# A decode-attention kernel: FFN and most of wo in column tiles, the loop's code moved by a block's remainder, unused matmuls in small loops

## The chip, the cores and the metric

The kernel runs on one core of one Trainium2 chip. The metric is the device time of one execution in microseconds (us), here the median of four: 660.58 (659.37 to 661.59). "The profile" is one more execution taken with the hardware profiler, and a line such as L275 is line 275 of that kernel's source. TensorE is the matmul engine (PE; its weight loads are PEld), VectorE is DVE, ScalarE is ACT, GpSimd is POOL and SyncE is SP; SP issues nearly all transfers.

## The reference

One decoding step of a transformer layer with a cached attention and a feed-forward network (FFN) side by side, both on the same normalised input. There are 2 sequences, one new token each, width 512, 32 heads of 128, 8192 cached positions, FFN width 1792, all in bf16.

```python
xn = _layernorm(x)                                   # (2, 1, 512)
q = (xn @ wq).reshape(2, 1, 32, 128)                 # per head
scores = q . k_cache * 128 ** -0.5                   # k_cache (2, 32, 8192, 128)
o = softmax(scores) . v_cache
out = x + o.reshape(2, 1, 4096) @ wo + relu(xn @ w1) @ w2
```

The two caches are 134 MB each, wq and wo 4 MB each, w1 and w2 1.8 MB each: 280.5 MB are read for 2 KB of output.

## The kernel before, in words

The 64 pairs of sequence and head are taken four at a time (`U = 4`), in `NP = 16` steps. For one step a K tile `ks` and a V tile `vs` are loaded, each 128 partitions by 64 KB (8 MB). There is one buffer of each, so K of the next step can be requested only when the transposes have read all of `ks`, and V of the next step only when the V matmuls have read all of `vs`. SP issues them in that order in `load` (L182): K waits for the semaphore `pT`, V for `sW`. The first and last K tiles, and the second and last V tiles, come in two halves.

Before the loop, x is normalised, wq is loaded into `vs`, and q is computed with 32 matmuls of 512 columns (L254). After that TensorE runs a hardware loop (`pe.Fori`) whose body is written out in full: 256 transposes of `ks` (L275) with VectorE and ScalarE copying the results to SBUF (`kT`, L429); 256 score matmuls (L282), with the maximum of each half of the scores found by VectorE (L476), transposed on TensorE (`turn`, L294) and spread to all partitions (`spread`, L300); ScalarE's exponentials (L550); 256 matmuls of V with the probabilities (L335, "PV"); and, except in the last two steps, 24 unused matmuls of 512 columns (L346) whose results nobody reads, at the end of the step.

Each step's softmax is scaled by its own maxima; the tail after the loop joins the halves. `RS` holds the sums, spread by four fp32 matmuls (L356), from which VectorE makes the factors, ending in `OTn` (L512). w1, w2 and wo are loaded into `ks`, after the last transposes: SP issues w1 (L190), w2 (L191), and wo in four pieces (L194) that follow `cuts = (0, 18, 26, 30, 32)`; a row `j` of `wo_sb` is 128 KB. TensorE first puts x into the output accumulator `fin` (L362), then does the FFN's first part with 56 matmuls, w1 as the weights and the two normalised tokens as the two moving columns (L373). It transposes `OTn` (L385), regroups it with four matmuls (L389), and then accumulates w2 (14 rows) and wo (32 rows) into `fin`, four matmuls a row with two moving columns each (`project`, L400, 184 in all). `fin` then holds the output with the 512 features spread over partitions; a copy `yT` (L526), a transpose (L420) and a copy `osb` (L528) lead to the output transfer (L196). On every engine the order is the order of the source: nothing is scheduled by a planner.

## Time and profile before

| what | value |
|---|---|
| median of 4 runs | 660.58 us |
| the profiled execution's own time | 660.51 us |
| its span, first to last instruction | 658.7 us |
| busy share of the span: PE, PEld, DVE, ACT, POOL | 90%, 82%, 40%, 44%, 1% |
| chain that ended last, by engine | DMA 49%, PE 48%, issue 1%, DVE 1% |
| DMA, mean over the span | 426 GB/s |
| mean granted TensorE clock | 0.981 |

The span is shorter than the execution's time by what lies before its first and after its last instruction. The chain is followed back from the last instruction to what released each step; it names one engine at a time, even where another ended nearly as late. "issue" is time in which an engine waited for nothing that the profile shows. Matmuls are pipelined: the duration of one record is longer than the distance from one to the next, so that costs are taken from a row's whole length divided by its count.

### The profile page before, as it was taken

How to read it: one execution, taken by the hardware profiler on the slowest of the kernel's cores; microseconds unless marked ns; L12 is line 12 of the kernel's file. 1: busy time of each engine (PE TensorE's matmuls, PEld its weight loads, DVE VectorE, ACT ScalarE, POOL GpSimd, SP SyncE). 2: the span in 40 equal slices, each digit the busy share in tenths (PEclk: the TensorE clock that was granted, in tenths of full speed). 3: DMA queues.
4: the chain of work that ended last, by engine and by line, in shares of the span. 5: the costliest groups of instructions: out<-in, count | busy, mean ns of one | idle time of the engine just before them, and what ended most of it. 6: DMA issues, size and time to landing. Idle time of an engine off the chain costs nothing.

```text
span 658.7 us, 27600 instructions
## 1 busy us (share of the span) xinstructions
PE 595.4 (90%) x12987; PEld 537.9 (82%) x12987; DVE 261.8 (40%) x503; ACT 290.7 (44%) x532; POOL 7.2 (1%) x30
## 2 busy tenths in 40 slices
PE   1876999999999899999989999998999999999997
PEld 0576897988879698887969878796987879798987
DVE  1440350716335071632507154260715416071721
ACT  1332452635445263543537354343725435372820
POOL 2000000000000000000000000000000000000000
PEclk9997898999999999999999999999999999999987
DMA  9999999999999999999999999999999999999996
GB/s 378 447 440 436 393 448 394 438 446 438 402 442 438 446 442 398 442 434 446 446 410 430 442 438 446 406 434 446 430 446 422 422 446 434 442 438 398 444 412 270
DMA packets 6223, 280.66 MB, mean 426 GB/s; under 512 B 706, under 2 KB 708, under 8 KB 964
## 3 DMA queue, kind: packets, MB, share of 16 engines
q1 hardware_dynamic: 6208, 280.50, 98.8%
q8 instruction: 8, 0.13, 0.1%
q14 instruction: 3, 0.02, 0.0%
q10 hardware_dynamic: 4, 0.00, 0.0%
HBM read 280.50 MB, written 0.00 MB: 426 GB/s over the span
## 4 chain that ended last, share of the span: by engine, by line
DMA 49%; PE 48%; issue 1%; DVE 1%; ACT 0%; SPq 0%; ACTq 0%
DMA ks<-in_A_k_cache_dram 49%; PE tp L275 34%; PE ot L335 6%; PE Sc L282 5%; PE ms L346 2%; PE Sc L400 1%; DVE mcol L476 1%; PE ms L373 1%; PE ms L294 0%; ACT L429 0%; ACT kT L429 0%; PE Sc L356 0%; PE ms L300 0%; SPq L182 0%; SPq L170 0%
## 5 line engine op out<-in xcount | busy, mean ns | idle before, releaser
L429 DVE COPY kT<-tp 128x1024 bf16<-128x1024 bf16 x320 | 209.2, 687 | 247.5 <-PE tp L275 241.8
L275 PEld LDWEIGHTS tp<-identb,ks 128*128 128x128 bf16 x4096 | 228.9, 98 | 23.6 <-DMA ks<-in_A_k_cache_dram 21.3
L275 PE MATMUL tp<-identb,ks 128*128 128x128 bf16 x4096 | 231.8, 219 | 16.7 <-DMA ks<-in_A_k_cache_dram 15.2
L429 ACT COPY kT<-tp 128x1024 bf16<-128x1024 bf16 x192 | 188.1, 1014 | 127.9 <-PE tp L275 127.9
L282 PE MATMUL Sc<-q,kT 128*128 128x64 bf16 (+8 forms) x4096 | 133.4, 191 | 4.8 <-issue 4.8
L335 PE MATMUL ot<-prm,vs 128*128 128x64 bf16 x4096 | 134.8, 195 | 2.2 <-issue 2.2
L335 PEld LDWEIGHTS ot<-prm,vs 128*128 128x128 bf16 x4096 | 130.8, 99 | 4.2 <-issue 2.3
L282 PEld LDWEIGHTS Sc<-q,kT 128*128 128x128 bf16 x4096 | 128.8, 98 | 6.3 <-issue 5.1
L346 PE MATMUL ms<-identb 128*128 128x512 bf16 x336 | 75.0, 380 | 0.0
L476 DVE TENSOR_REDUCE mcol<-Sc 32x1 bf16<-32x128 f32 x128 | 37.1, 290 | 94.4 <-PE Sc L282 93.1
L550 ACT ACTIVATE prm<-Sc,nm 32x128 bf16<-32x128 f32 x128 | 68.9, 538 | 5.4
L545 ACT COPY nm<-ms 128x4 f32<-128x4 f32 x32 | 5.2, 163 | 140.7 <-PE ms L300 140.7
L346 PEld LDWEIGHTS ms<-identb 128*128 128x128 bf16 x336 | 32.0, 98 | 36.6 <-issue 0.3
L561 ACT COPY OTf<-ot 128x8 f32 x16 | 2.6, 165 | 74.7 <-PE ot L335 74.7
L550 ACT ACTIVATION_READ_ACCUMULATOR prm<-Sc,nm x128 | 32.0, 250 | 0.0
L294 PE MATMUL ms<-identb,mcol 128*1 128x128 bf16 x32 | 7.0, 218 | 22.1 <-DVE mcol L476 22.1
L429 ACT ACT_TABLE_LOAD x16 | 20.5, 1283 | 3.7 <-issue 3.6
L294 PEld LDWEIGHTS ms<-identb,mcol 128*1 128x1 bf16 x32 | 2.5, 79 | 23.9 <-issue 23.1
L254 PE MATMUL ot<-vs,xz 128*16 128x512 bf16 x32 | 9.7, 477 | 8.8 <-DMA vs<-in_A_wq_dram 8.8
L254 PEld LDWEIGHTS ot<-vs,xz 128*16 128x16 bf16 x32 | 3.3, 106 | 14.8 <-issue 12.7
L483 DVE TENSOR_REDUCE mx<-ms 1x4 bf16<-1x128 bf16 x32 | 8.9, 279 | 13.8 <-PE ms L294 13.8
L236 POOL COPY q<-qb 128x4 bf16<-128x4 bf16 x16 | 3.0, 186 | 592.4 <-PE Sc L282 572.6
(61 smaller groups left out, 46.6 us busy)
## 6 DMA issues: line engine op xcount, KB each, us to landing
ks<-in_A_k_cache_dram SPq DMA_DIRECT2D x4, 4096.0 KB, 23.0
vs<-in_A_v_cache_dram SPq DMA_DIRECT2D x4, 4096.0 KB, 21.5
vs<-in_A_wq_dram SPq DMA_DIRECT2D x1, 4096.0 KB, 12.5
ks<-in_B_w_dram SPq DMA_DIRECT2D x2, 1792.0 KB, 16.5
ks<-in_A_wo_dram SPq DMA_DIRECT2D x1, 2304.0 KB
ks<-in_A_wo_dram SPq DMA_DIRECT2D x1, 1024.0 KB, 26.1
ks<-in_A_wo_dram SPq DMA_DIRECT2D x1, 512.0 KB, 26.9
ks<-in_A_wo_dram SPq DMA_DIRECT2D x1, 256.0 KB, 27.0
```

Source lines behind the costliest of these rows:

```text
L254: i = pe.matmul(qp, lhsT=xz[:, kt, Z - g * Bsz:Z - g * Bsz + QG * Bsz], rhs=vs[:, (kt * QG + g) * 512:(kt * QG + g + 1) * 512], start=(g = ...
L275: t = pe.transpose(tp[e % 4][:, i, :], ks[:, kk * Dh:(kk + 1) * Dh], identb[:])
L282: t = pe.matmul(Sc[:, U * kk:U * (kk + n)], lhsT=kT[e][:, i, :], rhs=rep(q4[:], n), start=True, stop=True,)
L294: pe.transpose(trp[:, i * P:(i + 1) * P], mcol[:, i:i + 1], identb[:]).then_inc(sT, 1)
L335: t = pe.matmul(oh[:, i, :], lhsT=vs[:, kk * Dh:(kk + 1) * Dh], rhs=rep(prm[:, kk, :], REP), start=(first == 0), stop=(first == KB // 2 - 1),)
L346: pe.matmul(ms[:], lhsT=identb[:], rhs=identb[:].rearrange("p (o k) -> p o k", o=1).to_broadcast([P, 4, P]), start=True, stop=True,)
L373: i = pe.matmul(hp[:, j, :], lhsT=w1_v[:, kt, j, :], rhs=xz[:, kt, Z:Z + Bsz], start=(kt == 0), stop=(kt == KT - 1),)
L400: t = pe.matmul(fin[:, k * Bsz:(k + 1) * Bsz], lhsT=w[:, j, k * P:(k + 1) * P], rhs=x[:, j, :], start=False, stop=(last and k == KT - 1),)
L429: fn(kT[e][:], tp[e % 4][:]).then_inc(kR[e % HG], 1)
L476: m = v.tensor_reduce(out=mcol[own, i:i + 1], in_=S[own, i * KB // 2:(i + 1) * KB // 2, u], axis=AX.X, op=ALU.max,)
L483: v.tensor_reduce(out=mx[:, i, :], in_=trp[:, i * P:(i + 1) * P].rearrange("o (u m) -> o u m", u=U), axis=AX.X, op=ALU.max, negate=True,). ...
L550: x = a.activation(out=prm[own, k, u], in_=S[own, k, u], func=ACTF.Exp, bias=nm[own, i, u:u + 1], scale=1.0, accum_out=RS[own, i, bass.ds( ...
```

## The change

- **Column tiles.** The FFN and rows 0 to 23 of wo change the roles of their operands. The activations become the weights, padded from 2 to `CT = 32` columns, and a row of w1, w2 or wo is moved through as 512 columns. A matmul then writes 32 output partitions, and four such outputs (`tile(ap, c)`) lie side by side in the 128 partitions of a PSUM bank. w1 takes 16 matmuls, w2 14, wo's rows 0 to 23 take 24. The hidden layer comes out with tokens along partitions, so ScalarE copies it to SBUF (`hb`), TensorE transposes it in four matmuls into `tp[3]`, and VectorE's relu writes `hT`. The sums `y` of the four column tiles are copied to SBUF in fp32 (`ys`), and four fp32 matmuls with `sel2` add the four tiles and turn them into `fin`. The last 8 rows of wo are done as before, 32 matmuls into `fin`. `hT` and `OX` are zeroed by GpSimd, as their padding is read; `OX`, `hb` and `ys` lie in the `kT` buffers, `hp` and `y` in the PSUM of the transposes.
- **Pieces.** The wo pieces are cut at 24 instead of 26.
- **50 matmuls ahead of q.** They are unused, 128 columns each, and stand before the wait for wq; the loop's code moves by 100 instructions.
- **Unused matmuls.** A step's 24 become a small hardware loop of 2 x 5, followed by one of 3 x 5 that is left out in step one: 25 in a step, 10 in step one.

The diff, without unchanged sizes and waits:

```diff
-WARM = 24
+EARLY = 50
+CT = 32
+    TC = P // CT
+    QW = 512 // P
+    first_j = [min(c * QW, FJ - QW) for c in range(TC)]
-    xz = sb([P, KT, 2 * Z + Bsz], bf16, "xz")
+    xz = sb([P, KT, max(2 * Z + Bsz, Z + CT)], bf16, "xz")
+    sel2 = sb([P, Bsz], f32, "sel2")
-    cuts = (0, 18, 26, 30, WJ)
+    cuts = (0, 18, 24, 30, WJ)
+    WIDE = 2
...
+        g.memset(hT[:], 0.0).then_inc(sI, 1)
...
+        g.wait_ge(sS, 2 * NP)
+        g.memset(OX, 0.0).then_inc(sI, 1)
...
+        for i in range(EARLY):
+            pe.matmul(ms[:, 0:P], lhsT=identb[:], rhs=identb[:], start=True, stop=True)
         pe.wait_ge(sV, 6)
         pe.wait_ge(dQ, 16)
...
+        def warm(n):
+            with pe.Fori(0, n):
+                for i in range(5):
+                    pe.matmul(ms[:], lhsT=identb[:], rhs=..., start=True, stop=True)
...
             with pe.If_lt(reg, NP - 1):
-                for i in range(WARM):
-                    pe.matmul(ms[:], lhsT=identb[:], rhs=..., start=True, stop=True)
+                warm(2)
+                with pe.If_ne(reg, 1):
+                    warm(3)
...
-        for j in range(FJ):
-            for kt in range(KT):
+        for kt in range(KT):
+            for c in range(TC):
                 i = pe.matmul(
-                    hp[:, j, :],
-                    lhsT=w1_v[:, kt, j, :],
-                    rhs=xz[:, kt, Z:Z + Bsz],
+                    tile(hp, c),
+                    lhsT=xz[:, kt, Z:Z + CT],
+                    rhs=w1_v[:, kt, first_j[c]:first_j[c] + QW, :],
...
+        pe.wait_ge(sF, 2)
+        for i in range(QW):
+            t = pe.transpose(tp[3][:, i, :], hb[:, i * P:(i + 1) * P], identb[:])
...
         for j in range(FJ):
-            project(w2_sb, j, hT)
+            c = j % TC
+            pe.matmul(
+                tile(y, c), lhsT=hT[:, slot[j], :], rhs=w2_sb[:, j, :],
+                start=(0 < j < TC), stop=False,
+            )
         pe.wait_ge(sV, 110)
-        for c in range(NC):
-            pe.wait_ge(*piece[c])
-            for j in range(cuts[c], cuts[c + 1]):
-                t = project(wo_sb, j, OX, j == WJ - 1)
+        for i in range(WIDE):
+            pe.wait_ge(*piece[i])
+            for j in range(cuts[i], cuts[i + 1]):
+                t = pe.matmul(
+                    tile(y, j % TC), lhsT=OX[:, j, :], rhs=wo_sb[:, j, :],
+                    start=False, stop=(j >= cuts[WIDE] - TC),
+                )
         t.then_inc(sH, 1)
+        for i in range(WIDE, NC):
+            if i == WIDE:
+                pe.wait_ge(sF, 5)
+                for k in range(KT):
+                    pe.matmul(
+                        fin[:, k * Bsz:(k + 1) * Bsz],
+                        lhsT=ys[:, k * P:(k + 1) * P],
+                        rhs=sel2[:],
+                        start=(k == 0),
+                        stop=False,
+                    )
...
+        v.tensor_copy(ys, y).then_inc(sF, 1)
...
+        a.wait_ge(sF, 1)
+        a.copy(hb, hp).then_inc(sF, 1)
```

On VectorE the relu moves behind the copy `Ob`, with a wait for the four transposes.

## The prediction

> **What bounds the kernel now.** I read the order of the chain of waits first, because the page's shares (DMA 49%, PE 48%) are averages over stages with different limits. From step three on, every turn of the loop is the same pair: 24.16 us waiting for a K tile, 14.48 us of transposes that set its buffer free for the next request. The stage table (its last three columns are TensorE's clock, the DMA's busy share and GB/s) and the list of waits say why:

> ```profile
> 200.00:400.00 200.00, 187.18 (x4122) 169.66 (x4120) 85.19 (x159) 94.88 (x170) 0.93 (x5) 1.00 1.00 434
> ```
> ```profile
> PE tp L275 <- DMA ks<-in_A_k_cache_dram: 15.2, 13, 1.7
> ```

> Between 200 and 400 us the DMA is never idle and moves 434 GB/s; one step is 16.8 MB (a K and a V tile of 128 x 64 KB each), which at that rate is 38.7 us, the measured turn. There the DMA is the limit, and TensorE has 15.2 / 13 = 1.2 us of slack a step. Only two stretches are not like that.

> The first is steps one and two. From the chain in order of time (start, us, what):

> ```profile
> 41.20 1.52 PE Sc L282 x49
> 42.72 1.16 issue
> 43.88 4.04 PE Sc L282 x127
> 47.91 0.15 PE ms L294
> 48.06 3.66 issue
> ...
> 63.64 2.21 issue
> 65.85 3.98 PE ot L335 x84
> 69.84 5.41 PE ms L346 x24
> 75.25 14.29 PE tp L275 x256
> ...
> 114.08 14.31 PE tp L275 x256
> ...
> 128.41 23.49 DMA ks<-in_A_k_cache_dram
> ...
> 166.44 24.16 DMA ks<-in_A_k_cache_dram
> ```

> Here TensorE is the chain. Three "issue" rows are holes in which it waits for nothing that the profile names, in its first pass through the loop only. Between two of them lie 127 score matmuls and one transpose, 128 pairs of weight load and matmul, 256 instructions. The DMA table for two stretches shows the code queue, q8 (packets, MB, share):

> ```profile
> q8 instruction: 4, 0.07, 0.8%
> ```
> ```profile
> q8 instruction: 2, 0.03, 0.7%
> ```

> The second stretch is the end (chain, the page's list of DMA issues, and the timeline's row of the four wo requests):

> ```profile
> 650.47 5.01 PE Sc L400 x184
> ```
> ```profile
> ks<-in_A_wo_dram SPq DMA_DIRECT2D x1, 1024.0 KB, 26.1
> ...
> ks<-in_A_wo_dram SPq DMA_DIRECT2D x1, 256.0 KB, 27.0
> ```
> ```profile
> 626.46 1.88 SPq L194 DMA_DIRECT2D ks<-in_A_wo_dram  x4
> ```

> The chain names TensorE alone, but the last wo piece, asked for at 627.9, lands 27.0 us later at 654.9, and the last matmul row ends at 655.48. The two end within 0.6 us of each other. A faster tail on TensorE alone can therefore win only some tenths.

> **The change part by part.**

> *Step one, 10 unused matmuls for 24.* K tile 1 was asked for at 41.23 and took 31.9 us: it lay there at 73.1, but its transposes began at 75.25, behind the unused ones (5.41 us for 24, 0.225 each). Fourteen fewer are 3.2 us, of which 2.15 are usable: then the landing is the limit. So K tile 2 is asked for near 87.4, not 89.57. What that is worth: tile 2 landed at 89.57 + 22.3 = 111.9, tile 3 at 128.41 + 23.49 = 151.9. From tile 1 that is 78.8 us for two turns where 2 x 38.7 = 77.4 would do. 1.4 us of DMA time were lost because requests came too late, and the whole stream behind, the tail too, was late by it. Bounds: 1.4 us gained; at the other end 0.3 lost, if TensorE, idle before 73.1, runs the transposes at a lower clock (the stage table has 0.75 for 50 to 70 us) and asks no earlier. I take 1.1 gained, nearer the full value, because the request moves by more than the loss.

> *The block shift.* Counting back 256 instructions at a time from the hole at 42.72, the old blocks begin 49.5 pairs into the loop; 100 new instructions put a block's first instruction at the loop's first. The loop then touches seven blocks, as before, and the one fetched ahead is the eighth. In step one a block took 7.8 us from hole to hole (43.88 to 51.72); the scores begin at 41.2 as before, and four block changes at 7 to 7.8 us put the end of PV at 69 to 72 us, a little less where a block was asked for ahead, against 69.84: no term, and ten unused matmuls still end about when tile 1 lands. The 50 matmuls themselves run from about 5 to 10 us, under the wait for wq that ends at 13.56 us: nothing; without that cover 5.3 us, at 0.107 each (a quarter of the 0.427 us between L254's first 512-column matmuls).

> *Unused matmuls in loops, 25 a step.* One more is 0.216 us (5.18 / 24) inside 1.2 us of slack: nothing. The branch: the jump into L346 at 69.84 and the jump back at 75.25 follow the row before them without idle time, so five more, each under 1.08 us of queued matmuls, cost 0; at the other end 0.15 us each (the gap at 610.05, where the loop turns with no unused matmuls), 0.75 a step, which the slack just takes. They also shorten the code.

> *Code fetches.* One more block is fetched in step one, and in the tail one or none before the last landing, for two. A block on one DMA engine (434 / 16 = 27 GB/s) is 0.6 us. [...]

> *FFN and wo in column tiles.* In the old run's time. Removed: L362 (0.18), 56 w1 matmuls (3.45), 184 narrow ones (5.01). RS ends at 645.96. Sixteen w1 matmuls of 512 columns follow; no row shows column tiles, so they are bounded by 0.216 each one after another (3.46) and a quarter of it side by side (0.86). I take the latter, as the four write different partitions with their own weights: 646.8. The copy hb on ScalarE (half of L429's 1.01) is done at 647.5. The transposes of OTn wait for VectorE's 648.20, not for w1; Ob (0.28), four transposes, the relu (0.19, now queued behind Ob on VectorE) lead to w2 at about 649.2, for 650.47 before. 14 + 18 wide matmuls take 1.7 us (to 6.9): 650.9. Now the next wait: piece 1, two rows shorter. The old one was asked for at 626.95, landed at 653.05; two rows are 256 KB, 0.6 us: 652.4. Six wide matmuls 0.32, their drain 0.17, the copy ys 0.68 (nearest row L458, 512 columns from PSUM), four fp32 matmuls 1.02 (L356, the same weight size), 32 narrow ones at 5.01 / 184 = 0.027 each 0.87. That ends at 655.5, against 655.48: the tail gains nothing by itself; I count 0.1 lost. Bounds: 0.4 gained (only the last landing counts), 1.0 lost (half clock in the tail, which the old run has from about 651 us, 0.50 in the stage table's last stretch).

> *Without cost:* sel2's reduction and the larger xz memset lie before wq's 13.4 us; the hT memset precedes a 19.7-us wait of GpSimd; the OX memset (0.95, L227's size) runs from 634 us, its reader comes at 648. SP's queue has as many requests.

> [...]

> **Rivals.**

> *The gain does not arrive.* The clock falls while TensorE waits for tile 1, K tile 2 is asked for no earlier, and the tail's chain behind piece 1 (3.1 us) shows: 660.6, up to 661.6 at half clock. For it: step one has clock 0.75 and the new wait falls there. Against: the window before the transposes still holds ten matmuls.

> *Column tiles run one after another (slower).* w1 then ends at 649.4 and w2 starts near 650.5; 38 wide matmuls take 8.2 us, and with 2.7 us of drain, copy, fp32 and narrow work the end is at 661.4, 6.0 late, 4.7 after the 1.3 gained: 665.2. From (652.7 - 649.2) / 38 = 0.09 us a wide matmul the tail loses, from 0.13 it has eaten the 1.3. For it: no row of the old run shows overlap. Against: disjoint columns and outputs.

> *The loop no longer fits.* The new block start coincides with the loop start within one or two instructions of my count. If the jump lands one instruction before it, the loop needs nine blocks with the one ahead, and if eight is all that is held (the old run needed just eight), each step costs what step one's pass did: 24.87 to 69.84 less 1.7 of waiting for K, and 5.4 of unused matmuls, is 48.7 for 38.7; 14 x 10 makes about 800.

> *The small loops cost more than the slack,* say 0.2 us a step beyond it: 14 x 0.2 = 2.8 against 1.2, 662.1.

> **How the numbers follow.** The profiled execution took 660.51 us (span 658.7 and 1.8 around it), 0.07 under the median of 660.58. -1.1 - 0.2 + 0.1 = -1.2: 659.3. A measurement of this kernel tells about 0.2%, 1.3 us, from no change, so this is just at the edge. Chances: my forecast 0.62, its own range 658.2 to 660.0; no gain 0.22; serial tiles 0.08; no fit 0.04; loop cost 0.04. Faster: 0.45 from the forecast. Same: its other 0.17 and 0.14 of the second case. Slower: 0.24. Bounds summed give -2.4 to +1.9, 658.1 to 662.4 with the median's own spread of a few tenths at the low end: 657.7 to 662.3, which leaves out the serial tiles and the loop that does not fit.

> **What would show it.** Right: transposes of tile 1 near 73.1, turns of 38.7 from tile 2 on, no q8 packets from 75 to 640 us, wide matmuls well under 0.1 us apart, fp32 rows waiting behind a copy. Wrong: wide matmuls 0.216 apart, "issue" holes in later steps, K waits shrunk to nothing, or tile 2 asked for at 89 us again.

## The result, and the profile after

The change makes the kernel a little slower. Its median is 661.84 us (42 executions, 658.6 to 664.14) against 659.72 for the kernel before (67 executions, 658.15 to 667.29), and the ratio is 1.002 with a 95% interval of 1.0011 to 1.003, that is 0.7 to 2.0 us. The medians differ by 2.1 us, the means by 1.3: of the 42 executions 9 lie at 658.6 to 659.7, the rest from 660.2 up. The forecast was 659.3, faster. The range held the time, the direction was wrong.

The profiled execution of the kernel after took 660.69 us (span 658.9), 0.2 more than the profiled one of before, and 1.2 less than its own median: it is one of the quicker ones. It shows the new wait, though not yet what that costs in most executions. Its chain in order of time (start, us, what):

```profile
41.20 3.85 PE Sc L299 x127
45.06 1.47 issue
...
50.99 2.84 issue
...
61.37 1.91 issue
63.27 4.03 PE ot L361 x128
67.30 3.38 issue
70.67 0.50 PE ot L361 x6
71.18 3.29 PE ms L324 x10
74.47 14.31 PE tp L292 x256
88.79 24.04 DMA ks<-in_A_k_cache_dram
112.88 14.48 PE tp L292 x256
...
166.05 24.16 DMA ks<-in_A_k_cache_dram
```

Before, step one had three "issue" holes, 7.0 us together. Now there are four, 9.6 us, and the new one stands before the last six PV pairs: 3.38 us of waiting for 0.50 us of work. PV therefore ends at 71.2, the ten unused matmuls at 74.5, 1.7 us after K tile 1 landed (72.8), and K tile 2 is asked for at 88.8, not at the forecast 87.4. The steady turn is unchanged (24.16 and 14.48 us), as the stage table and the list of waits say too:

```profile
200.00:400.00 200.00, 188.26 (x4132) 170.16 (x4130) 84.86 (x158) 94.52 (x170) 0.93 (x5) 1.00 1.01 435
```
```profile
PE tp L292 <- DMA ks<-in_A_k_cache_dram: 14.3, 14, 1.9
```

The code queue has five packets from 42 to 76 us, none from 76 to 655, and one after that:

```profile
q8 instruction: 5, 0.08, 0.9%
```

The tail (chain of the same kernel):

```profile
645.58 3.77 PE tp L391 x16
...
650.69 1.04 PE tp L427 x14
651.73 1.33 PE tp L435 x22
653.07 0.02 issue
653.09 0.70 DVE kT L578
653.79 0.04 issue
653.84 1.05 PE Sc L444 x8
654.89 0.81 PE Sc L454 x32
```

The 38 wide matmuls of w2 and wo take 2.4 us and the 32 narrow ones that stay 0.81, where 184 narrow ones took 5.01; the sum over the four tiles (copy, four fp32 matmuls) gives that back; and w1's 16 wide ones take 3.77, where 56 narrow ones took 3.45. The last narrow row ends at 655.70, against 655.48. Seen from the landing of the last wo piece (654.7 us, before 654.9) that is 1.0 us behind it, for 0.6 before.

**One measure serves for all runs below.** K tile 3 should land two turns, 77.4 us, after K tile 1. What it takes beyond that is DMA time lost in steps one and two. In the profile of before that was 78.81 - 77.4 = 1.41, in the one after 78.72 - 77.4 = 1.32. These two profiles thus differ by next to nothing in this measure; what the new wait costs is seen against the kernels below that lose less than 0.1, and in the other profiles with the same code shift.

### The profile page after: what moved, and what is told of

Its sections match the earlier page's. It is cut to its first block, busy times and chain, and to the rows that moved or that the text cites. A ratio compares the mean times of both kernels' runs of the same rounds, so it can differ in the third digit from the quotient of the medians.

```text
span 658.9 us, 27588 instructions
## 1 busy us (share of the span) xinstructions
PE 598.2 (91%) x12891; PEld 534.6 (81%) x12891; DVE 262.6 (40%) x505; ACT 291.3 (44%) x533; POOL 8.6 (1%) x32
## 4 chain that ended last, share of the span: by engine, by line
DMA 52%; PE 44%; issue 2%; DVE 1%; ACT 0%; SPq 0%; ACTq 0%
DMA ks<-in_A_k_cache_dram 52%; PE tp L292 34%; PE ot L361 4%; PE Sc L299 4%; PE tp L391 1%; DVE mcol L525 1%; PE ms L324 0%; PE tp L435 0%; ACT L472 0%; PE ms L311 0%; PE Sc L444 0%; PE tp L427 0%; ACT kT L472 0%; PE Sc L379 0%; PE Sc L454 0%
## 5 line engine op out<-in xcount | busy, mean ns | idle before, releaser
L361 PE MATMUL ot<-prm,vs 128*128 128x64 bf16 x4096 | 132.8, 194 | 5.3 <-issue 5.3
L361 PEld LDWEIGHTS ot<-prm,vs 128*128 128x128 bf16 x4096 | 128.6, 98 | 7.3 <-issue 5.5
## 6 DMA issues: line engine op xcount, KB each, us to landing
ks<-in_A_wo_dram SPq DMA_DIRECT2D x1, 256.0 KB, 27.2
```

What stands on the lines that cost most here:

```text
L361: t = pe.matmul(oh[:, i, :], lhsT=vs[:, kk * Dh:(kk + 1) * Dh], rhs=rep(prm[:, kk, :], REP), start=(first == 0), stop=(first == KB // 2 - 1),)
```

## The experiments

Ratios are to the kernel before, run on the same chip. The theories at first were: that the loss is the tail's (A, B) or step one's (C), and within step one that it comes through the clock (K), from the code's place among the 16-KB blocks (M) or from the small loops (L).

### Each part alone

*e1: the column tiles alone,* with the old unrolled unused matmuls and nothing ahead of q.

```diff
-        for i in range(EARLY):
-            pe.matmul(ms[:, 0:P], ...)
-                warm(2)
-                with pe.If_ne(reg, 1):
-                    warm(3)
+                for i in range(24):
+                    pe.matmul(ms[:], ...)
```

> The column tiles and the new pieces alone; the loop, its 24 unused matmuls and the code's place are those of the kernel before. Theory A (the new tail is longer, and longer still in executions in which TensorE's clock is halved there): +1.0 to +2.5 us against before, with a wider spread of its times than before. Theory C (the loss is in step one, from the 50 matmuls and the small loops): within 0.4 us of before.

659.83 us, 1.0002 (0.9989 to 1.0014): no difference.

*e2: the other half,* the kernel before with the 50 matmuls and the small loops (the diff of the change's loop part alone).

> The 50 matmuls ahead of q and the small loops alone; the tail is that of before. Theory A: -0.6 to +0.3 us against before. Theory C: +1.0 to +2.0 us.

663.02 us, 1.0043 (1.0027 to 1.0058). The loss is here. Not all of it is step one's: in this run alone the median time exceeds the span by 2.8 us, where before and all other kernels have 1.8, and the trace has a code packet at 662.6, behind the span's end at 660.9. By spans the loss is 2.35 us (660.3 against 657.95), much as in e6 below (2.55).

*e8: the small loops alone,* e2 without the 50.

```diff
-        for i in range(EARLY):
-            pe.matmul(ms[:, 0:P], ...)
```

> The kernel before with the small loops alone (25 unused matmuls a step, 10 in step one); no 50 matmuls, the old tail. If the small loops are harmless, and the 10 in step one bring K tile 2's request forward as predicted: 0.5 to 1.5 us under before. If they cost: over before.

659.21 us, 0.9998 (0.9981 to 1.0016), with single executions from 658.7 to 664.2. The small loops cost nothing that can be told apart.

*e5: the kernel after without the 50* (the same two lines taken out of it).

> The changed kernel without the 50 matmuls ahead of q. Theory K (the 50 matmuls warm TensorE's clock early, so q ends earlier, TensorE then sits idle long enough before K tile 0's second half that its clock falls, and everything in step one up to the request of K tile 2 comes late): the second half's 128 transposes take 7.3 us, K tile 2 is asked for before 89 us, and the time is 1.5 to 3 us under the changed kernel, 0.3 to 1.5 under before. Theory M (the code's new place among the 16-KB blocks is what costs): also under the changed kernel; e6 and e7 tell the two apart. Theory L (the small loops cost): as the changed kernel.

659.52 us, 0.9997 (0.9985 to 1.0009). With column tiles and small loops, and without the 50, the kernel is as before. So all of the loss comes with the 50 matmuls ahead of q, which the forecast had put at nothing. In its profile PV ends four microseconds after its last hole, before tile 1 lands, and the chain is the landing (timeline rows, then chain):

```profile
66.07 4.19 PE L359 MATMUL ot<-prm,vs 128*128 128x64 bf16 x84 [2.74 <-issue]
70.10 2.32 PE L322 MATMUL ms<-identb 128*128 128x512 bf16 x10
```
```profile
41.44 31.40 DMA ks<-in_A_k_cache_dram
72.84 0.05 issue
72.88 14.47 PE tp L290 x256
87.35 5.39 PE Sc L297 x176
```

### The 50 matmuls, or the place they give the code

*e6: the 50 stand in the code, and a jump passes over them.* TensorE executes none.

```diff
+        never = nc.alloc_register(mybir.EngineType.PE, "never")
+        pe.reg_mov(never, 1)
+        with pe.If_lt(never, 1):
-        for i in range(EARLY):
-            pe.matmul(ms[:, 0:P], ...)
+            for i in range(EARLY):
+                pe.matmul(ms[:, 0:P], ...)
```

> The changed kernel with the 50 matmuls in the code but jumped over: the loop starts within two instructions of the same place, and the clock is not touched. Theory K: as e5, 1.5 to 3 us under the changed kernel. Theory M: as the changed kernel, 1 to 3 us over before.

661.9 us, 1.003 (1.0017 to 1.0043): the whole loss, with nothing executed.

*e7: the 50 are executed, as ten turns of a loop over five,* so that the code moves by some 14 instructions, not 100.

```diff
-        for i in range(EARLY):
-            pe.matmul(ms[:, 0:P], ...)
+        with pe.Fori(0, EARLY // 5):
+            for i in range(5):
+                pe.matmul(ms[:, 0:P], ...)
```

> The changed kernel with the same 50 matmuls run as 10 turns of 5: the clock is touched as in the change, and the code moves by 14 instructions instead of 100. Theory K: as the changed kernel, 1 to 3 us over before, with some half-clock transposes of K tile 0's second half (8.6 us instead of 7.3). Theory M: as e5.

659.76 us, 0.9998 (0.9985 to 1.001): all of the work, none of the loss. It is the place, not the work. The timeline rows of e7 have no wait behind 65.73, and PV ends at 68.6:

```profile
65.73 2.91 PE L362 MATMUL ot<-prm,vs 128*128 128x64 bf16 x91 [3.01 <-issue]
68.47 2.32 PE L325 MATMUL ms<-identb 128*128 128x512 bf16 x10
```

The chain of e6 shows the fourth hole again:

```profile
65.87 4.02 PE ot L364 x128
69.90 3.10 issue
72.99 0.56 PE ot L364 x7
73.55 4.27 PE ms L327 x10
77.81 14.83 PE tp L295 x256
```

*e9 and e10: other distances.* In place of the 50, a jump over 20 pairs, and one over 113 (the same diff as e6, with `range(20)` and `range(113)`). The code moves by 42 and by 228 instructions.

> The changed kernel, but in place of the 50 executed matmuls a jump over 20 pairs that are never executed, so that all later TensorE code moves by about 42 instructions instead of 100. Theory M (what costs is that the loop's last PV pairs come to lie in one further 16-KB block, a fourth block change on step one's path): with 42 the loop's last instruction still lies within the block that holds it in the unshifted kernel, so the time is as without the 50 matmuls, 659.5 us within 0.5, the end of PV in step one at 66 to 70 us, and K's third tile asked for before 90. Theory S (any shift costs, in proportion to its length): about +0.9 us over the kernel before, 660.5. Theory J (the jump itself costs, since the jump over 50 pairs gave 661.9): 661.9 again.

> The changed kernel, but in place of the 50 executed matmuls a jump over 113 pairs that are never executed: all later TensorE code moves by about 228 instructions, nearly a whole block of 256, so that the block boundaries lie against the loop about 28 instructions before where they lie without any shift. Theory M (place within the blocks, not the length of the shift): the loop crosses as many blocks in step one as unshifted, PV ends near 68 us, and the time is 659 to 660.5 us. Theory S (in proportion to the shift): 2.3 times the loss of 100, +4.5 us, about 664. Theory J (the jump): 661.9.

659.85 us, 0.9999 (0.9983 to 1.0014), and 659.34, 0.9995 (0.9984 to 1.0006). Neither costs anything, although one moves the code by more than twice as much as the change does. The theories of length and of the jump fall; M holds: it depends on where the boundaries cut the loop. The chains (e9, then e10):

```profile
41.18 31.58 DMA ks<-in_A_k_cache_dram
72.76 0.05 issue
72.81 16.09 PE tp L295 x256
```
```profile
41.48 31.32 DMA ks<-in_A_k_cache_dram
72.80 0.05 issue
72.85 14.48 PE tp L295 x256
87.35 24.21 DMA ks<-in_A_k_cache_dram
```

What the boundaries do is seen in the starts of the q8 packets, one block each (16,384 bytes in the traces of before and after; starts read from the trace, us):

```
shifted by 100 (after)   29.5  36.8  44.1  51.5  60.9  68.2  75.4
shifted by 100 (e6)      28.1  36.7  47.0  53.6  63.4  70.4  77.9
not shifted    (e5)      30.9  41.8  48.9  56.3  63.6  70.4
shifted by 42  (e9)      28.2  39.3  46.6  53.8  61.0  68.2
shifted by 228 (e10)      9.1  31.9  41.8  49.0  55.8  63.1  70.6
```

With the DMA full (0.97 busy from 42 to 76 us in after), most blocks follow each other at 7 us or a little more (6.6 at the least), whereas 128 pairs, 256 instructions, run in 4.03 us. So the time of step one is counted in blocks. Shifted by 100, the loop's end needs a block more between 27 and 78 us than at the other distances; at 228 the additional block comes at 9.1, under the wait for wq. The last packet in a row starts only after PV has ended (75.4 against 71.2 in after, 77.9 against 73.6 in e6, and 70.4 against 69.8 in before), so it seems to bring a block ahead of need.

### From the late end of PV to the time

*e11: the kernel after, with no unused matmuls in step one.*

```diff
-                warm(2)
                 with pe.If_ne(reg, 1):
-                    warm(3)
+                    warm(5)
```

> The changed kernel with its 50 early matmuls and its shift, but no unused matmul in step one (10 before). The block change ahead of the last PV pairs stays (PV ends near 71 us), and only the 3.3 us of the loop of ten behind it go. Theory M2 (the loss is the late start of tile 1's second transposes and so the late request for K's third tile): they begin when PV ends or the tile has landed, 71.5 to 73 us instead of 74.5, K's third tile is asked for before 88, and the time falls by 1 to 2 us against the changed kernel's 661.8, to 660 to 660.8. Theory M3 (the loss lies in something else that the shift moves, such as later fetches): 661.8 within 0.5. A rival within M2: with no unused matmul the clock falls to half before the transposes, which then last 25 us instead of 14.5, and the time is above 664.

660.87 us, 1.0018 (1.0007 to 1.0029): the median is 1.0 lower than the kernel after's 661.84 and just above theory M2's range (up to 660.8), but the ratio is the same, so it settles nothing. What the ten had cost came back as a slower clock: it was 0.73 from 72 to 77 us, where the kernel after had 1.00 at the start of its transposes (74.5 to 79 us), and the transposes took 16.09 us instead of 14.31.

```profile
72.92 0.35 PE ot L361 x6
73.28 0.83 issue
74.11 16.09 PE tp L292 x256
```

*e14: the opposite, 25 unused matmuls in step one,* in the kernel after; *e13: the same in e5,* the kernel without the 50.

```diff
-                with pe.If_ne(reg, 1):
+                with pe.If_ne(reg, 0):
```

> The changed kernel with its shift and its 50 early matmuls, and with 25 unused matmuls in step one in place of 10. Theory R (the time follows the request for K's third tile): PV ends at 71 to 73.5 us, 25 matmuls end at 76.5 to 80, the request goes out at 91 to 95 instead of 88.8 to 92.7, and the time is 1 to 2.5 us above the changed kernel's 661.8: 663 to 664.5. Theory N (the shift costs by something else): 661.8 within 0.5.

> The changed kernel without the 50 early matmuls, and with 25 unused matmuls in step one as in every other step, in place of 10. Theory R (the time follows the request for K's third tile): unshifted, PV ends at 66 to 70 us, 25 matmuls of 0.216 us end at 71.5 to 75.5, tile 1 has landed at 72.8 and is transposed at full clock, so the request goes out at 87.3 to 90 and the time is 659.5 us within 0.5, as with ten: the ten of step one were worth nothing. Theory G (the gain of ten, 1.1 us, is there as the prediction had it, in the kernel without the shift): 660.2 to 660.7.

e14: 663.07 us, 1.0059 (1.0039 to 1.0078), 1.2 above the kernel after. In its chain the 25 end at 78.6, K tile 2 is asked for at 92.9, and steps one and two lose 3.94 us of DMA time. Theory R holds and N falls:

```profile
72.82 0.35 PE ot L361 x6
73.17 5.45 PE ms L324 x25
78.62 14.29 PE tp L292 x256
```

So unused matmuls that end later behind the late PV cost time. That the kernel after's own loss goes this way, with ten, is argued from the profiles and not measured by itself, as e11 did not settle it.

e13: 660.38 us, 1.0011 (0.9996 to 1.0027), 0.9 above e5. That median is in theory G's range (660.2 to 660.7) and not in R's (up to 660.0); but the intervals of e13 and e5 overlap, so that what ten are worth against 25 in the unshifted code is between nothing and about 1 us.

Over all profiles the request for K tile 2 and the DMA time lost in steps one and two go together, though loosely: before and e8 both ask at 89.57 and lose 1.41 and 2.61, so the request is not all that sets the loss.

| runs | K tile 2 asked for at | lost, us |
|---|---|---|
| e1, e5, e10 | 87.3 to 87.4 | 0.07 to 0.09 |
| e13 | 88.3 | 0.99 |
| after, e9, e12, e7 | 88.8 to 89.0 | 1.32, 0.65, 2.22, 0.76 |
| before, e8, e3, e15 | 89.6 to 90.0 | 1.41, 2.61, 2.57, 2.65 |
| e11, e2 | 90.2, 91.4 | 0.95, 2.37 |
| e4, e6, e14 | 92.6 to 92.9 | 2.93, 3.07, 3.94 |

Each row is one profiled execution, and some lie far from their kernel's median (e8 at 662.29, median 659.21; e15 at 662.51, median 660.54).

In the seven profiles with the shift PV ends at 71.2 to 73.6 us, in the nine of experiments without it, and in before, at 66.0 to 70.3. The kernel after's own profile, with 71.2, is the best of the seven; the other six have a lower clock in tile 0's second transposes (0.57 to 0.68 from 33 to 37 us, for 1.00), and so begin the scores 1.3 to 1.8 us later. The clock is the last column but two in the stage table (after, then e6):

```profile
33.00:37.00 4.00, 3.12 (x56) 3.12 (x57) 1.96 (x3) 2.13 (x3) 0.00 (x0) 1.00 1.19 512
```
```profile
33.00:37.00 4.00, 3.23 (x36) 3.24 (x37) 1.38 (x2) 1.18 (x2) 0.00 (x0) 0.68 1.15 496
```

That may be why some executions of the kernel after reach 658.6 and most do not; it is not shown, as none of the fastest was profiled. But the slower clock alone is not what the change costs: e7 had 0.52 in that stretch, and no loss, and e7, e13 and e15, unshifted and slow there too (0.52 to 0.73), ended PV at 68.5 to 69.8.

### The tail

*e3: w1 read contiguously.* The kernel after, with w1's columns taken in runs of 512 (h comes out in another order, and w2's rows are loaded to match, in pieces of 1 KB).

```diff
-        sp.dma_start(w2_sb, B_w2.rearrange("(p j) n -> p j n", j=FJ))
+        sp.dma_start(w2_sb, B_w2.rearrange("(j p) n -> p j n", j=FJ))
-                    rhs=w1_v[:, kt, first_j[c]:first_j[c] + QW, :],
+                    rhs=w1_sb[:, kt, first_j[c] * P:(first_j[c] + QW) * P],
```

> The changed kernel with w1 moved through in 512 neighbouring columns instead of columns 28 bytes apart; w2's rows are laid out to fit, in 1-KB runs. Theory B (the 28-byte step is what makes a round of four w1 matmuls 0.91 us instead of 0.22, and it decides): the w1 matmuls take about 1 us instead of 3.8, w2 starts near 649, and the time is 0.5 to 1.5 us under the changed kernel. If the transfers decide instead: w1 is quicker, but the time stays within 0.4 us of the changed kernel, or is above it, as w2's short runs load 0.6 us longer.

664.65 us, 1.0066 (1.0049 to 1.0083): slower than the kernel after. Between 600 and 645 us, when w2's short pieces come, the DMA moves 417 GB/s in its profile, and 426 to 430 in the others: that is about 1 us (0.6 had been expected, from no run), and not all of the difference. But the price of w1's stride is plain, in the timeline rows of the kernel after and of e3:

```profile
645.51 3.82 PE L391 MATMUL tp<-ks,xz 128*32 128x512 bf16 x16
```
```profile
646.69 1.05 PE L390 MATMUL tp<-ks,xz 128*32 128x512 bf16 x16
647.66 0.39 PE L398 MATMUL tp<-xsb,identb 2*32 2x512 bf16 x1
```

Contiguous, sixteen take 0.97 us (646.69 to 647.66), 0.24 for four side by side. With a step of 28 bytes from element to element (14 bf16) the next operation starts 3.75 us later, 0.94 for four: 3.9 times as long.

*e4: the old 56 narrow matmuls for w1,* in the kernel after; *e12: the same without the 50 ahead of q.*

```diff
-                    tile(hp, c),
-                    lhsT=xz[:, kt, Z:Z + CT],
-                    rhs=w1_v[:, kt, first_j[c]:first_j[c] + QW, :],
+                    hp[:, j, :],
+                    lhsT=w1_v[:, kt, j, :],
+                    rhs=xz[:, kt, Z:Z + Bsz],
```

> The changed kernel with the FFN's first part as before (56 matmuls with w1 as weights), w2 and wo in column tiles. Theory B: w1 takes 3.45 us, hT is there without the copy and the four transposes, w2 starts about 0.5 us earlier, and the time is 0.3 to 1 us under the changed kernel. Theory A, as far as the wide w2 and wo matmuls carry the half clock: still 0.5 us or more above before, with a wide spread.

> The changed kernel without the 50 early matmuls, and with the old w1 (56 narrow matmuls whose result has h transposed already, so without the copy and the transposes of h). Without the 50 alone it took 659.5. Theory T (the end is set by the last pieces of wo, and w1 in column tiles costs nothing although its rounds of four take 0.91 us): 659.5 within 0.4. Theory B (the 3.8 us of w1's 16 matmuls lie on the path of the end): 1 to 2 us faster, 658 to 658.5.

e4: 662.93 us, 1.0035 (1.0017 to 1.0052). e12: 661.4, 1.0024 (1.0011 to 1.0038), where e5, with w1 in column tiles, had 659.52. Undoing the slow part of the tail gains nothing; the strided w1 is not what the change loses by, and theories A and B fall. That e12 is slower than e5 nobody had expected. In its profile the two turns after K tile 3 take 39.56 and 38.87 us for 38.7, another 1.0 us lost, and the cause of that stays open.

*e15: e12 with 25 unused matmuls in step one* (the diff of e14).

> The changed kernel without the 50 early matmuls, with the old 56 narrow matmuls of w1, and with 25 unused matmuls in step one. With ten it took 661.4, although the loop stands where it stands in the kernel that took 659.5. Theory H (with ten, TensorE stands idle before tile 1's second half and is granted half the clock, and the late request that follows costs): 659.5 within 0.5, the transposes 14.5 us at full clock. Theory W (narrow w1 beside column tiles of w2 and wo costs by itself, in the tail): 661.4 within 0.5. Theory D (the DMA ran slower between 150 and 250 us in that run by chance, whatever the kernel): between 659.3 and 661, with single runs of both kinds.

660.54 us, 1.0017 (0.9998 to 1.0036), with single executions from 659.2 to 664.9. The transposes had the full clock; the turn after K tile 3 took 39.13 us, 0.4 too long. The median is above theory H's range (up to 660.0), in D's and below W's (660.9 to 661.9), but the interval reaches into all three, so the run decides little. What slowed e12 stays open; e2, e6 and e8, with other tails or another place of the code, have 39.1 to 39.3 in the same turn, and e8 no loss in its median.

Why the tail gains nothing is seen in e1, whose stream was not late (0.08 lost). Its wide matmuls wait for a piece of wo (timeline rows):

```profile
650.48 0.61 PE L436 MATMUL tp<-ks,kT 128*32 128x512 bf16 x6 [0.41 <-DMA ks<-in_A_wo_dram]
651.87 1.05 PE L445 MATMUL Sc<-sel,kT 128*128 128x2 f32 x8 [0.79 <-DVE kT L579]
652.79 0.97 PE L455 MATMUL Sc<-kT,ks 128*128 128x2 bf16 x32
```

## Why the prediction was wrong, point by point

**The step that failed is "The block shift".** It counted the boundaries rightly: a block's first instruction at the loop's first, seven blocks, four block changes in step one, the end of PV at "69 to 72 us". PV ended at 71.2 in the profile, and at 73.2 to 73.6 in the other six with the shift, where the scores did not begin at 41.2, as the forecast had it, but at 42.5 to 43.0. It then set that against 69.84 and wrote "no term". Two things were wrong in this. The comparison was with one sample: in the nine profiles of experiments without the shift PV ends at 66.0 to 70.3, and 69.84 is near the late end. And a range whose upper end lies behind the landing of K tile 1 is a term: after 70.6 the ten unused matmuls (2.2 us at full clock) end later than the landing at 72.8, and the transposes and the next request come late. The runs put it at the whole loss: e6 against e7, 661.9 against 659.76, with e9 and e10 to show that the place decides and not the distance.

**"Step one, 10 unused matmuls for 24"**: 1.1 us gained, forecast; the wait was there, but not the gain. Where PV ends early enough, the request for K tile 2 does go out at 87.35 to 87.4 (e5, e10), and the 1.4 us of lost DMA time are gone (0.07 to 0.09). But the kernel before probably loses them only in some executions: its profiled one, 660.51, and the four of which 660.58 was the median lie about 1 us above the median of its 67, 659.72, which is where e5 and e10 are too. It was profiled once, so this is not shown. e1, with 24 unused matmuls, asks at 87.3 as well when PV ends at 66.3. And where PV ends early, ten are too few for the clock: with gaps of 2.1 to 4.8 us before tile 1's transposes (e7, e8, e9, e12) the clock from 72 to 77 us is 0.50 to 0.71, the transposes take 16.1 to 16.6 us, and the request is late again; with gaps of 0.5 and 1.4 us (e5, e10) it is 1.00, and they keep 14.5. The lower bound of the step (0.3 lost by a slower clock) had this case.

**"Unused matmuls in loops"**: 0, and 0 was measured (e8: 0.9998). "It fits" was right as well: no q8 packet from 76 to 655 us. **"Code fetches"**, 0.2 gained in the tail: no run shows this term. A packet's record lasts about 1 us (0.93 to 1.08 in before and after), for the 0.6 of the sum; the kernel after has one fetch at 655.7, behind the last landing (654.7), before had two ahead of it (648.7 and 652.7, landing 654.9); e1 and e5 show no gain that could be told apart.

**"FFN and wo in column tiles"**: 0.1 lost, forecast; e1 says 1.0002 (0.9989 to 1.0014). The sum came out near, with one term far off: w1's sixteen took 3.75 us for 0.86, so w2 began at 650.69 instead of 649.2; that lay in front of the wait for the pieces of wo, which took up all but 0.2 us. The rest came as forecast: ys 0.69 (0.68), fp32 1.05 (1.02), the narrow row 0.81 (0.87). Seen from the last landing the tail ends 0.4 us later than before, which e1's interval cannot tell from nothing.

**The rivals.** "Column tiles run one after another" falls: four start within 10 ns and the next four 0.22 us later, and 22 of them take 1.33 us. "The loop no longer fits" falls (no q8 packet from 76 to 655 us; how many blocks are held at the most no run shows), and so does "The small loops cost more than the slack" (e8: 0.9998). "The gain does not arrive" (660.6, up to 661.6) came nearest, but by a clock or the tail; the cause was neither. (The summed bounds end at 662.4, the stated range at 662.3.)

**Wide matmuls and block changes in numbers.** The 38 wide matmuls take 2.37 us in the chain (1.04 and 1.33), for the 2.1 that a quarter of 0.216 each had given. The loop jumps back over its seven blocks in every step, and no q8 packet is seen from 76 to 655 us: none of the later passes fetches code. In the first pass, with the DMA at 416 GB/s (42 to 76 us, kernel after), the block changes left the holes of 1.2 to 3.7 us that the two chains show.

## What to carry to other kernels

Code that is run once while the DMA is as full as here (416 GB/s) should be counted in 16-KB blocks, not in instructions: each block cost about 7 us from fetch to fetch, and six pairs that spilled into one more block cost 3.4 us of waiting. Before an end time is called harmless, put its range against the event behind it (a landing, a request), and take the range from several executions, since one profile may be a late one. A faster tail is worth only what its last transfer leaves free (e1: nothing, 1.0002), and unused matmuls at the head of the kernel can be put into a loop, or their place padded by a jump (e7, e9 and e10: 0.9995 to 0.9999), so that the place of the code behind them is a choice of its own.

## What the hardware showed that was not expected

- Instructions that are never executed can cost 2 us: e6 jumps over 50 pairs and is 0.3% slower, while jumping over 20 or 113 is free (0.9999 and 0.9995).
- Column tiles do run side by side, but not at any stride: 0.24 us for four matmuls of 512 contiguous columns, 0.94 at a step of 28 bytes, although narrow matmuls with the same w1 as weights take 0.062 each (3.45 / 56).
- The time that is lost by late requests in steps one and two is never made up: from the landing of K tile 3 to that of the first half of the last K tile it is the same 454.8 us in before, after, e1, e5, e7, e9, e11, e13 and e14, whatever was lost ahead of it (0.08 to 3.94 us), and more, 455.0 to 455.8, in the other eight.
